# A gated linear attention with a channel mix on one core: the first two 128-token groups as one of 256, no separate load of the fourth head pair, and dummy products in the planned TensorE gaps up to the first mix

## The chip, the core and the metric

The kernel runs on one core of a Trainium2 chip. The metric is the device time of one execution in microseconds (us), the median of several runs. TensorE is called PE here (PEld is its weight load), VectorE DVE, ScalarE ACT, GpSimd POOL and SyncE SP. SP does no arithmetic here: it issues the transfers.

## What is computed

Two stages follow each other. The first is a recurrence over 768 tokens, for 4 sequences and 8 heads of 48 features, with a 48x48 state for each head:

```python
for t in range(S):
    state = alpha[:, :, t, :, None] * state + np.einsum('bhd,bhe->bhde', k[:, :, t], v[:, :, t])
    y[:, :, t] = np.einsum('bhd,bhde->bhe', q[:, :, t], state)
```

The second takes y with the heads side by side as x (4, 768, 384) and mixes each token with the one before it:

```python
xk = mu_k * x + (1.0 - mu_k) * x_prev
xr = mu_r * x + (1.0 - mu_r) * x_prev
k = np.maximum(xk @ w_k, 0.0)          # 384 -> 1024
v = k * k @ w_v                        # 1024 -> 384
out = 1.0 / (1.0 + np.exp(-(xr @ w_r))) * v
```

## The kernel before, in words

**Groups and chunks.** A sequence is cut into chunks of C = 128 tokens, and the chunks into attention groups (`CUTS`, L29). Before, the first sequence is cut 1, 1, 2, 2 and the others 2, 2, 2, so there are 13 groups and 24 chunks. `PLACE` (L32) says in which of two buffers a group's alpha, q, k and v lie and at which half of it: the two one-chunk groups share buffer 0. `MOES` (L34) says which groups one channel mix takes: the first mix takes groups 0 and 1 (256 columns), the second group 2 (256), the other five two groups each (512).

**Preparing a group** (`attention_inputs`, L313). SP loads alpha, q, k and v. DVE scans alpha forward for each head pair (`forth`, L364), multiplies q by the products (`times`, L391), takes a reciprocal (`turn`), scans backward (`back`, L406) and multiplies k. The rows hold three head pairs in full, and the fourth pair's 96 features lie as 16 further rows of each of the three. Group 0 alone is in `DIRECT` (L33): it has its fourth pair loaded once more into its own place (`extra`, L331, six transfers for alpha, q and k), and its scans run over four pairs. Every other group scans three pairs, and SP gathers the fourth pair of the finished q and k by transfers within the core's memory (`gather`, L428, two each, and `small`, L441, two for the decay at the group's end).

**Products of a chunk** (`attention_products`, L626). TensorE transposes k (`trans`), ACT copies it out (`keep`). For the first `JOINED` = 4 chunks the products come in two jobs: `enter` (state growth and scores, 64 + 64 instructions in the profile, which shows each float32 product as two) and, after DVE has masked the scores (`masked`) and advanced the state (`advance`), `visit` (output). Later chunks join the visit of one with the entry of the next. ACT copies the output (`leave`), DVE adds a part (`crossed`), and SP spreads the fourth pair (`spread`, L576).

**The channel mix.** `mix_jobs` (L861) forms xk and xr: for each of three feature blocks ACT scales, DVE blends, ACT rounds to a high part and DVE takes the low part. `up_jobs` (L894) makes eight products blocks, each of 9 PE products (high x high, low x high, high x low, three blocks each), and after each one ACT's `relu`, `square` and `whole` and DVE's `low`. `gate_jobs` makes three blocks of 9, `down_jobs` three of 24, closed by DVE and stored by SP. The up blocks, gates and downs of all mixes form one chain on PE in program order (`pe_job`, L890); only attention jobs can go between. In the first mix `up_jobs` is called for each of the two segments (L1007), so there are 16 up blocks of 128 columns, planned with a factor 1.6 (`slow`, L895); its gates and downs are 256 wide.

**Weights.** w_k, w_r and w_v come in 10 pieces through two raw buffers (`weights`, L729, `RAWS` = 2): SP loads (L739), ACT takes the top bits (L744), DVE joins (L752), ACT makes the high part (L760), DVE the low one (L764), and then the buffer is free for the piece after next.

**What sets the order.** Every step is a job of a `Plan` (L67) with a planned duration, and `plan.order` lists the jobs by planned start after 60 rounds of list scheduling. Each engine and SP then runs its own jobs in that order, whatever the true durations are. At the head of PE's stream 22 dummy products of zeros are issued (`WARM`, L52). While the planned start is below `QUIET` = 45 us, dummies also fill PE's planned gaps from the first job on:

```python
if plan.start[j] < QUIET and at > 0.0:
    for i in range(int((plan.start[j] - at - 0.2) / 0.2)):
        PE.matmul(pms[2][:R, :R], zero, zero, start=True, stop=True)
at = plan.start[j] + plan.dur[j]
```

A dummy is two PE instructions in the profile (L235 and L1057).

Of the kernel before, what the change touches and what calls it, by code (L numbers as in the profile page):

```python
# [25 lines left out]
B, H, S, D = 4, 8, 768, 48  # L26
DM, FF = 384, 1024
C = 128
CUTS = [[1, 1, 2, 2], [2, 2, 2], [2, 2, 2], [2, 2, 2]]  # L29
GROUPS = [(b, sum(cut[:i]), n) for b, cut in enumerate(CUTS) for i, n in enumerate(cut)]  # L30
NA = len(GROUPS)
PLACE = [(0, 0), (0, 1)] + [(i, 0) for i in range(1, NA - 1)]  # L32
DIRECT = (0,)  # L33
MOES = [[0, 1], [2], [3, 4], [5, 6], [7, 8], [9, 10], [11, 12]]  # L34
NG = len(MOES)
LMAX = 2 * C
WMAX = 2 * LMAX
NP = H // 2
# [4 lines left out]
NT = 3  # L43
# [5 lines left out]
DW = D // DQ  # L49
NX = HB - D  # L50
NW = 768
WARM = 22  # L52
ROUNDS = 60
RAWS = 2
JOINED = 4
QUIET = 45.0


def head(i, o):
# [120 lines left out]
def mm(n):  # L180
    return 0.013 + n / 2400.0 if n > 128 else 0.068
# [6 lines left out]
def act(n, extra=0.0):  # L188
    return 0.13 + n / 1200.0 + extra
# [7 lines left out]
def gated_attention_channel_mix(  # L197
# [17 lines left out]
    PE, ACT, DVE, POOL, SP = nc.tensor, nc.scalar, nc.vector, nc.gpsimd, nc.sync  # L215
# [21 lines left out]
    als, pps, ks, qs = (ring(x, 2, [128, NP * LMAX]) for x in ("al", "pp", "k", "q"))  # L237
    vs = ring("v", 2, [C, 2 * VW])
    for t in (als[0], ks[0], qs[0]):
        POOL.memset(t[:, NT * C : NP * C], 1.0)  # L240
    tiny = cp.tile([128, 1], F32, name="tiny")
    POOL.memset(tiny, FLOOR)
    mone = cp.tile([128, 1], F32, name="mone")
# [32 lines left out]
    tops = [early[:, :NW], *ring("tops", 1, [128, NW], U32)]  # L276
# [19 lines left out]
    plan = Plan()  # L296
    add = plan.add
# [12 lines left out]
    loads, prepped, gathered, half_k, half_q, rescale = {}, {}, {}, {}, {}, {}  # L310
# [150 lines left out]
    def final(a):  # L461
        return a + 1 == NA or GROUPS[a + 1][0] != GROUPS[a][0]

    def trans(i):
        a, c = CH[i]
        k = view(a, ks)
        for p in range(NT):
            PE.transpose(pt[:, p, :], k[:, p, c * C : (c + 1) * C], ident)  # L468
# [141 lines left out]
    def advance(i):  # L610
        a, c = CH[i]
        old, new, nxt = before[i, 0], before[i, 1], marks[i]
        DVE.tensor_tensor(by_pair(new), by_pair(old), grown[:R, 0], op=ALU.add)
        if nxt is None:
            return
        DVE.tensor_tensor(by_pair(nxt), by_pair(new), grown[:R, 1], op=ALU.add)
        if c == GROUPS[a][2] - 1:
            DVE.tensor_tensor(
                by_pair(nxt), by_pair(nxt), pes[a % 2][:R].unsqueeze(2).to_broadcast([R, NP, D]),
                op=ALU.mult,  # L620
            )
# [4 lines left out]
    def attention_products():  # L626
        last_mask = last_leave = last_cross = last_adv = last_visit = None
        done = {}
        tcopy = {}

        def slow(i):
            return 1.3 if i < JOINED else 1.0

        def joined_at(i):
            return i >= JOINED

        for i in range(-1, NCH):
            more = i + 1 < NCH
            need = [last_mask, last_adv, last_leave, last_cross, last_visit]
            opened = ()  # L640
            if more:
                a, c = CH[i + 1]
                tr = add(
                    "PE", 0.32 * slow(i), lambda i=i: trans(i + 1), need=[prepped[a]],
                    takes=[("pt", i + 1)], uses=[("k", a)], name=f"trans{i + 1}",
                )

                def keep(i=i):
                    ACT.copy(hts[(i + 1) % 2].rearrange("t (r i) -> t i r", i=NT), pt)  # L649

                tcopy[i + 1] = add(
                    "ACT", act(NT * 128, -0.02), keep, need=[tr], takes=[("ht", i + 1)],
                    uses=[("pt", i + 1)], name=f"ht{i + 1}",
                )
                ready = [tcopy[i + 1], *half_k[a], *half_q[a], *loads[a]["v"]]
                touched = [("ht", i + 1), ("k", a), ("q", a), ("v", a)]
                opened = (0,) if marks[i + 1] is None else (0, 1)
            if i >= 0:
                mine = [("am", i), ("q", CH[i][0]), ("v", CH[i][0]), *before[i]]
            joined = i >= JOINED and more  # L660

            def visit(i=i, out=i >= 0, more=more, opened=opened if joined else ()):
                if more and joined_at(i):
                    update(i + 1, opened)
                if out:
                    intra(i, opened)
                    inter(i, 0)
                    inter(i, 1)
                if more and joined_at(i):
                    scores(i + 1)  # L670

            def enter(i=i, opened=opened):
                update(i + 1, opened)
                scores(i + 1)

            vis = None
            if i >= 0:
                need += ready if joined else []
                vis = add(
                    "PE", (2.28 if joined else 1.5) * slow(i), visit, need=need,  # L680
                    uses=mine + (touched if joined else []), name=f"visit{i}",
                )
                last_visit = vis
                a, c = CH[i]
                last_leave = add(
                    "ACT", 0.5, lambda i=i: leave(i), need=[vis], takes=[("xt", slot_of[a])], name=f"leave{i}"
                )
                last_cross = add(
                    "DVE", 0.42, lambda i=i: crossed(i), need=[vis, last_leave], uses=[("xt", slot_of[a])],
                    name=f"cross{i}",  # L690
                )
                done.setdefault(a, []).append(last_cross)
            if more and not joined:
                a, c = CH[i + 1]
                vis = last_visit = add(
                    "PE", 1.0 * slow(i), enter, need=[*ready, last_mask, last_adv, last_leave, last_cross, last_visit],
                    uses=touched, name=f"enter{i + 1}",
                )
            if more:
                last_mask = add(  # L700
                    "DVE", 0.62, lambda i=i: masked(i + 1), need=[vis], takes=[("am", i + 1)],
                    name=f"mask{i + 1}",
                )
                a, c = CH[i + 1]
                ending = c == GROUPS[a][2] - 1
                last_adv = add(
                    "DVE", 0.62 + (0.25 if ending and not final(a) else 0.0), lambda i=i: advance(i + 1),
                    need=[vis, last_adv, *(rescale.get(a, ()) if ending else ())],
                    takes=[("st", x) for x in held[i + 1]],
                    uses=[before[i + 1][0], *([("pe", a)] if ending else [])], name=f"state{i + 1}",  # L710
                )
            if i >= 0:
                a, c = CH[i]
                if c == GROUPS[a][2] - 1:
                    mv = add(
                        "SP", 0.2, lambda a=a: spread(a), need=done[a], uses=[("xt", slot_of[a])], name=f"spread{a}"
                    )
                    src = [] if GROUPS[a][1] == 0 else [done[a - 1][-1], xready[a - 1][0]]
                    pre = add(
                        "POOL", 0.25, lambda a=a: prefix(a), need=src, takes=[("xt", slot_of[a])],  # L720
                        uses=[("xt", slot_of[a - 1])] if src else [], name=f"prefix{a}",
                    )
                    xready[a] = [mv, *done[a], pre]


    converted = {}
    turn_w = [0]

    def weights(key, f, src, at, hi, lo):  # L729
        n = hi.shape[1] * hi.shape[2]  # L730
# [15 lines left out]
                raw.bitcast(BF16)[:, 4::4], AF.Copy,  # L746
            )

        hb = add("ACT", act(n), head_bits, need=[ld], takes=[("tops", i)], uses=[("raw", i)], name=f"top {key}{f}")

        def join():
            DVE.scalar_tensor_tensor(  # L752
# [139 lines left out]
        return j  # L892

    def up_jobs(g, n0, n, w, xr_):  # L894
        slow = 1.6 if g == 0 else 1.0  # L895
        for f in range(NF):
            i, pk = acc(n)
            ri = rn[0]
# [5 lines left out]
            def ops(f=f, pk=pk, r=r, k2=k2, dst=dst, xh=xh, xl=xl):  # L904
# [4 lines left out]

            prod, relu = up_ops(f, pk, xh, xl, r, k2, None, None)[:2]  # L910
            jp = pe_job(
                9 * mm(n) * slow, prod, [*xr_, *converted["k", f // 2]], takes=[("pm", i)], uses=[("xk", g)],
                name=f"up{g}.{f}+{n0}",
            )
            jr = add("ACT", act(n, -0.02), relu, need=[jp], takes=[("r", ri)], uses=[("pm", i)], name=f"relu{g}.{f}")
# [131 lines left out]
    for j in late:  # L1047
        plan.need[j] += [k for i in range(turn_w[0]) for x in ("tops", "raw") for k in plan.users[x, i]]

    todo = plan.order(sizes, ROUNDS)  # L1050
    POOL.tensor_scalar(nu, mu, -1.0, 1.0, op0=ALU.mult, op1=ALU.add)
    at = 0.0
    for j in todo:
        if plan.eng[j] == "PE":
            if plan.start[j] < QUIET and at > 0.0:
                for i in range(int((plan.start[j] - at - 0.2) / 0.2)):
                    PE.matmul(pms[2][:R, :R], zero, zero, start=True, stop=True)  # L1057
            at = plan.start[j] + plan.dur[j]
        plan.fn[j]()
    order.close()  # L1060

# [177 lines left out]
```

## Time and profile before

| what | us |
|---|---|
| median of 3 runs | 366.55 (364.83 to 367.21) |
| the profiled execution | 367.48 |
| its span, first to last instruction | 365.8 |
| PE busy in the span | 347.4 |
| DVE busy | 225.3 |
| ACT busy | 203.1 |
| start of the first up product | 33.57 |
| start of the first down product | 77.65 |

The profile shows one execution. Its times run from the span's start, and "busy" is the time in which an engine had an instruction in work. The granted clock is the share of TensorE's full speed that the chip gave: 1.00 is 2.4 GHz and 0.50 is 1.2 GHz.

### The profile page before, as it was taken

Reading aid. Unit: us, or ns where it says so; the run is one execution under the profiler, and the core shown is the slowest. Engines: PE = TensorE matmul, PEld = TensorE weight load, DVE = VectorE, ACT = ScalarE, POOL = GpSimd, SP = SyncE. Lnnn points to the kernel's source line nnn. Section 1 sums busy time; section 2 is a strip of 40 time slices with the busy share of each in tenths; the row PEclk is TensorE's granted clock in tenths of the full one; section 3 lists DMA queues with packets and bytes.
Section 4 is the critical chain, followed back from the end, with each engine's and each line's share of the span. In section 5 each row is a group of like instructions: output and inputs, shape, how many; then the busy total and the mean of one; then the engine's idle time right before and its main releaser. Section 6 shows DMA issues by size and latency. Waiting matters only on the chain. (4 is left out here: it accounts for less than half of the span.)

```text
span 365.8 us, 10482 instructions
## 1 busy us (share of the span) xinstructions
PE 347.4 (95%) x4469; PEld 301.1 (82%) x4469; DVE 225.3 (62%) x453; ACT 203.1 (56%) x405; POOL 24.6 (7%) x63
## 2 busy tenths in 40 slices
PE   7497999999999999999999999999999999999991
PEld 7387999999999888888888888888888888888780
DVE  5897566587898954659934679517479312743000
ACT  2756565455874993318981349951269731787100
POOL 6110021010000300100000010000000000000000
PEclk9798555599999999999999999999999999999997
DMA  5997705243644202543203443005421001100011
GB/s 182 319 316 227 232 2 185 55 143 82 175 112 125 77 6 62 161 161 90 78 3 104 135 142 110 18 2 126 144 68 39 2 3 42 40 29 0 4 59 35
DMA packets 18295, 35.62 MB, mean 97 GB/s; under 512 B 3776, under 2 KB 9408, under 8 KB 18240
## 3 DMA queue, kind: packets, MB, share of 16 engines
q1 hardware_dynamic: 18096, 34.86, 31.6%
q8 instruction: 37, 0.61, 0.7%
q14 instruction: 18, 0.15, 0.2%
q10 hardware_dynamic: 144, 0.00, 0.0%
HBM read 26.69 MB, written 4.72 MB: 86 GB/s over the span
## 5 line engine op out<-in xcount | busy, mean ns | idle before, releaser
L810 PE MATMUL pm<-xkh,wkh 128*128 128x512 f32 (+2 forms) x192 | 52.5, 388 | 1.6 <-ACT xkh L796 1.6
L810 PE MATMUL pm<-xkl,wkh 128*128 128x512 f32 (+2 forms) x192 | 51.5, 383 | 0.0
L810 PE MATMUL pm<-xkh,wkl 128*128 128x512 f32 (+2 forms) x192 | 51.5, 383 | 0.0
L810 PEld LDWEIGHTS pm<-xkh,wkh 128*128 128x128 f32 x192 | 37.6, 223 | 7.2 <-ACT xkh L796 2.0
L847 PE MATMUL pm<-kb,wvh 128*128 128x512 f32 x120 | 42.2, 404 | 0.0
L810 PEld LDWEIGHTS pm<-xkl,wkh 128*128 128x128 f32 x192 | 38.0, 224 | 4.9
L810 PEld LDWEIGHTS pm<-xkh,wkl 128*128 128x128 f32 x192 | 38.1, 224 | 4.9
L816 ACT ACTIVATE r<-pm 128x512 f32<-128x512 f32 (+2 forms) x64 | 31.1, 486 | 18.4 <-PE pm L810 18.1
L847 PE MATMUL pm<-kha,wvh 128*128 128x512 f32 (+1 forms) x108 | 38.1, 353 | 0.0
L847 PE MATMUL pm<-kla,wvh 128*128 128x512 f32 (+1 forms) x108 | 37.0, 342 | 0.0
L847 PE MATMUL pm<-kha,wvl 128*128 128x512 f32 (+1 forms) x108 | 36.8, 341 | 0.0
L790 ACT ACTIVATE x<-xt,mu 128x512 f32<-128x512 f32 (+2 forms) x48 | 26.3, 609 | 18.4 <-DMA xt<-xt 17.6
L582 DVE TENSOR_TENSOR am<-sp,mask 128x512 f32<-128x512 f32 x24 | 16.5, 688 | 31.6 <-PE sp L497 31.5
L822 ACT ACTIVATE k<-r 128x512 f32<-128x512 f32 (+2 forms) x64 | 32.6, 516 | 1.5 <-DVE kla L825 1.0
L649 ACT COPY ht<-pt 128x384 f32<-128x384 f32 x24 | 16.3, 678 | 30.3 <-PE pt L468 30.2
L793 DVE SCALAR_TENSOR_TENSOR x<-xt,nu,x 128x512 f32<-128x512 f32 (+2 forms) x48 | 27.3, 612 | 5.7 <-ACT x L790 4.9
L825 DVE TENSOR_TENSOR kb<-k,kb 128x512 fp32r<-128x512 f32 x20 | 13.8, 692 | 24.4 <-ACT k L822 14.9
L560 ACT COPY xt<-yu 112x512 f32<-112x512 f32 x24 | 14.0, 584 | 24.6 <-PE yu L535 20.5
L847 PEld LDWEIGHTS pm<-kb,wvh 128*128 128x128 f32 x120 | 22.6, 188 | 5.1
L970 DVE TENSOR_TENSOR sig<-pm,sig 128x512 f32<-128x512 f32 (+1 forms) x21 | 12.8, 611 | 22.3 <-PE pm L847 17.4
L409 DVE TENSOR_TENSOR_SCAN pp<-al,pp 128x255 f32<-128x255 f32 (+1 forms) x40 | 26.3, 690 | 0.3
L365 DVE TENSOR_TENSOR_SCAN pp<-al,tiny 128x256 f32<-128x256 f32 (+1 forms) x40 | 23.6, 630 | 3.3 <-DMA al<-al_p 1.7
(90 smaller groups left out, 630.4 us busy)
## 6 DMA issues: line engine op xcount, KB each, us to landing
v<-v_p SPq DMA_DIRECT2D x11, 400.0 KB, 5.1
al<-al_p SPq DMA_DIRECT2D x11, 384.0 KB, 3.2
q<-q_p SPq DMA_DIRECT2D x11, 384.0 KB, 3.8
k<-k_p SPq DMA_DIRECT2D x11, 384.0 KB, 3.7
out<-sig SPq DMA_DIRECT2D x15, 256.0 KB, 2.1
early<-wk_p SPq DMA_DIRECT2D x4, 768.0 KB, 4.5
early<-wv_p SPq DMA_DIRECT2D x4, 768.0 KB, 4.8
q<-q SPq DMA_DIRECT2D x22, 48.0 KB, 2.3
```

What stands on the lines that cost most here:

```text
L365: DVE.tensor_tensor_scan(view(a, pps)[:, p], view(a, als)[:, p], tiny.to_broadcast([128, n]), initial=START, op0=ALU.mult, op1=ALU.max,)
L409: DVE.tensor_tensor_scan(pp[:, p, 0 : n - 1][:, ::-1], x, x, initial=pp[:, p, n - 1 : n], op0=ALU.mult, op1=ALU.bypass,)
L560: ACT.copy(x[:R].rearrange("r i (s t) -> r i s t", s=2), yu[:R, :, : NP * HC].rearrange("r s (i t) -> r i s t", i=NP),)
L582: DVE.tensor_tensor(ams[i % 2], sp[:, :, : NP * HC].rearrange("c j (p t) -> c j p t", p=NP), mask.unsqueeze(1).unsqueeze(1).to_broadcast([ ...
L649: ACT.copy(hts[(i + 1) % 2].rearrange("t (r i) -> t i r", i=NT), pt)
L790: ACT.activation(x, now, AF.Copy, scale=mu[:, i, t : t + 1])
L793: DVE.scalar_tensor_tensor(x, prev, nu[:, i, t : t + 1], x, op0=ALU.mult, op1=ALU.add)
L810: PE.matmul(pk, w[:, t, cols], x[:, t], start=part == 0 and t == 0, stop=part == 2 and t == NT - 1,)
L816: ACT.activation(r, pk, AF.Relu)
L822: ACT.activation(k2, r, AF.Square)
L825: DVE.tensor_tensor(lo, k2, hi.bitcast(F32), op=ALU.subtract)
L847: PE.matmul(pv, w[f // 2][:, f % 2, cols], x, start=f == 0 and i == 0, stop=f == NF - 1 and i == 2,)
```

## The change

All four sequences are cut 2, 2, 2, so there are 12 groups, each of 256 tokens and each with a buffer half of the ring to itself. No group loads its fourth pair separately; group 0 gathers it as the others do. The first mix takes group 0, the second group 1, the rest two each. The first mix therefore calls `up_jobs` once, with 8 blocks of 256 columns. 20 dummies stand at the head. After them dummies fill every planned gap of PE, from planned time 8.6 on and with 0.19 us planned for one, up to the first job that writes the third accumulator (`filled`; the third up block of the first mix). Some planned durations change.

```diff
-CUTS = [[1, 1, 2, 2], [2, 2, 2], [2, 2, 2], [2, 2, 2]]
+CUTS = [[2, 2, 2]] * 4
-PLACE = [(0, 0), (0, 1)] + [(i, 0) for i in range(1, NA - 1)]
-DIRECT = (0,)
-MOES = [[0, 1], [2], [3, 4], [5, 6], [7, 8], [9, 10], [11, 12]]
+PLACE = [(i, 0) for i in range(NA)]
+DIRECT = ()
+MOES = [[0], [1], [2, 3], [4, 5], [6, 7], [8, 9], [10, 11]]
-WARM = 22
+WARM = 20
+WARMED = 8.6
-QUIET = 45.0
-        POOL.memset(t[:, NT * C : NP * C], 1.0)
+        POOL.memset(t[:, NT * LMAX :], 1.0)
-                    "PE", 0.32 * slow(i), lambda i=i: trans(i + 1), need=[prepped[a]],
+                    "PE", 0.26 * slow(i), lambda i=i: trans(i + 1), need=[prepped[a]],
-                    "ACT", act(NT * 128, -0.02), keep, need=[tr], takes=[("ht", i + 1)],
+                    "ACT", 0.61, keep, need=[tr], takes=[("ht", i + 1)],
-                    "DVE", 0.62 + (0.25 if ending and not final(a) else 0.0), lambda i=i: advance(i + 1),
+                    "DVE", 0.75 + (0.3 if ending and not final(a) else 0.0), lambda i=i: advance(i + 1),
-        hb = add("ACT", act(n), head_bits, need=[ld], takes=[("tops", i)], uses=[("raw", i)], name=f"top {key}{f}")
+        hb = add("ACT", act(n, 0.2), head_bits, need=[ld], takes=[("tops", i)], uses=[("raw", i)], name=f"top {key}{f}")
-        slow = 1.6 if g == 0 else 1.0
-                9 * mm(n) * slow, prod, [*xr_, *converted["k", f // 2]], takes=[("pm", i)], uses=[("xk", g)],
+                9 * mm(n), prod, [*xr_, *converted["k", f // 2]], takes=[("pm", i)], uses=[("xk", g)],
+    filled = set(plan.first["pm", 2])
-    at = 0.0
+    at = WARMED
+    cold = True
     for j in todo:
         if plan.eng[j] == "PE":
-            if plan.start[j] < QUIET and at > 0.0:
-                for i in range(int((plan.start[j] - at - 0.2) / 0.2)):
+            if cold:
+                for i in range(int((plan.start[j] - at) / 0.19)):
                     PE.matmul(pms[2][:R, :R], zero, zero, start=True, stop=True)
             at = plan.start[j] + plan.dur[j]
+            cold = cold and j not in filled
```

## Rows read from the trace of the kernel before

**Rows 1.** The page: busy time of each engine (share of the span, instructions), and the granted clock in 40 slices of 9.1 us, in tenths.
```profile
PE 347.4 (95%) x4469; PEld 301.1 (82%) x4469; DVE 225.3 (62%) x453; ACT 203.1 (56%) x405; POOL 24.6 (7%) x63
...
PEclk9798555599999999999999999999999999999997
```
**Rows 2.** Windows: the stretch, its length, then busy time and instructions of each engine in it, the granted clock, the busy share of the DMA engines and GB/s.
```profile
33.57:72.06 38.49, 38.49 (x344) 37.78 (x345) 24.57 (x64) 23.24 (x75) 3.67 (x3) 0.50 0.42 131
72.06:74.50 2.44, 2.44 (x12) 2.44 (x13) 1.80 (x2) 1.47 (x5) 0.00 (x0) 0.50 0.61 161
...
33.57:77.65 44.08, 44.08 (x435) 43.17 (x436) 28.72 (x70) 27.20 (x85) 3.67 (x3) 0.54 0.40 124
77.65:130.00 52.35, 52.13 (x870) 49.17 (x869) 47.73 (x101) 36.31 (x82) 6.63 (x9) 1.00 0.44 120
130.00:160.00 30.00, 30.00 (x560) 24.85 (x563) 15.17 (x31) 13.67 (x24) 1.27 (x4) 1.00 0.31 87
```
**Rows 3.** Timeline of PE in the first 34 us: start, length, what, and in brackets the idle time before it and what ended it.
```profile
14.58 0.87 PE L468 MATMUL pt<-ident,k 128*128 128x128 f32 x3 [6.50 <-DVE k L393]
...
16.22 0.97 PE L485 MATMUL yu<-v,ht 64*64 64x48 f32 x30
...
18.07 2.88 PE L1057 MATMUL pm<-zero 112*112 112x112 f32 x18
...
22.58 2.52 PE L1057 MATMUL pm<-zero 112*112 112x112 f32 x24
25.03 0.78 PE L485 MATMUL yu<-v,ht 64*64 64x48 f32 x30
...
27.79 0.34 PE L497 MATMUL sp<-q,k 48*64 48x64 f32 x6 [1.11 <-DMA k<-k]
...
30.89 1.04 PE L1057 MATMUL pm<-zero 112*112 112x112 f32 x8
33.57 0.91 PE L810 MATMUL pm<-xkh,wkh 128*128 128x128 f32 x3 [1.64 <-ACT xkh L796]
```
**Rows 4.** Timeline of PE, three products to a row: two neighbouring rows 128 columns wide, two 256 wide soon after, and two 256 wide later. The difference of two starts is what three products cost.
```profile
34.27 0.84 PE L810 MATMUL pm<-xkh,wkl 128*128 128x128 f32 x3
34.91 0.84 PE L810 MATMUL pm<-xkl,wkh 128*128 128x128 f32 x3
...
72.81 0.84 PE L835 MATMUL pm<-xrh,wrl 128*128 128x256 f32 x3
73.45 0.84 PE L835 MATMUL pm<-xrl,wrh 128*128 128x256 f32 x3
...
95.96 0.52 PE L810 MATMUL pm<-xkl,wkh 128*128 128x256 f32 x3
96.32 0.52 PE L810 MATMUL pm<-xkh,wkh 128*128 128x256 f32 x3
```
**Rows 5.** Timeline of PE: the entry of one chunk and what follows it, at 0.50 and at 1.00 of the clock.
```profile
47.76 0.97 PE L485 MATMUL yu<-v,ht 64*64 64x48 f32 x30
...
49.62 0.90 PE L810 MATMUL pm<-xkh,wkh 128*128 128x128 f32 x3
...
82.94 0.79 PE L485 MATMUL yu<-v,ht 64*64 64x48 f32 x30
...
84.22 0.38 PE L847 MATMUL pm<-kha,wvh 128*128 128x256 f32 x1
```
**Rows 6.** Groups by form: busy time, mean ns of one. The first two are of 33.57 to 79.01, the next of 79 to 113 on DVE and of 85 to 113 on ACT; the last two are timeline rows of ACT.
```profile
L822 ACT ACTIVATE k<-r 128x128 f32<-128x128 f32 x16 | 4.6, 301 | 0.0
...
L825 DVE TENSOR_TENSOR kla<-k,kha 128x128 fp32r<-128x128 f32 x16 | 4.3, 284 | 0.3 <-ACT k L822 0.3
...
L825 DVE TENSOR_TENSOR kla<-k,kha 128x256 fp32r<-128x256 f32 x8 | 3.2, 414 | 0.0
...
L822 ACT ACTIVATE k<-r 128x256 f32<-128x256 f32 x8 | 3.3, 409 | 1.1 <-DVE kla L825 1.0
...
30.86 0.96 ACT L790 ACTIVATE x<-xt,mu 128x128 f32<-128x128 f32 x3
...
84.56 1.31 ACT L790 ACTIVATE x<-xt,mu 128x256 f32<-128x256 f32 x3 [3.64 <-DMA xt<-xt]
```
**Rows 7.** The start. Timeline of SP (one of the three pairs of fourth-pair loads, then a gather of k), windows as in rows 2, and from the view of one line the times from issue to landing (least, median, most) up to 60 us, first of the gathers of q and k (L431), then of the spread (L579).
```profile
1.72 1.33 SPq L334 DMA_DIRECT2D al<-al_p  x2
...
21.57 1.21 SPq L431 DMA_DIRECT2D k<-k  x2
...
1.50:6.00 4.50, 4.50 (x26) 4.50 (x25) 2.05 (x6) 1.50 (x4) 4.16 (x19) 1.00 0.56 132
6.00:30.00 24.00, 16.24 (x294) 14.97 (x296) 20.15 (x39) 12.28 (x18) 3.92 (x8) 0.86 0.94 315
...
DMA to landing us min/median/max: 2.1/4.4/5.6
...
DMA to landing us min/median/max: 2.7/4.6/6.5
```
**Rows 8.** Timeline of DVE: forward and backward scans of one 256-token group, three pairs each.
```profile
77.86 1.85 DVE L365 TENSOR_TENSOR_SCAN pp<-al,tiny 128x256 f32<-128x256 f32 x3
...
100.69 2.02 DVE L409 TENSOR_TENSOR_SCAN pp<-al,pp 128x255 f32<-128x255 f32 x3
```
**Rows 9.** Waits of SP's queue: who was waited for, us in total, times, longest.
```profile
SPq L739 <- DVE wvl L764: 15.0, 2, 13.6
```

## The prediction

> **What bounds the kernel now.** I read the page first. PE is busy in 95% of the span, DVE in 62% and ACT in 56% [rows 1], so the whole asks for PE; but the line of the granted clock shows a hole. From slice 4 to slice 8, some 34 to 74 us, PE ran at the lower of its two clocks, 1.2 for 2.4 GHz [rows 1]. Then I cut that stretch out by windows. From 33.57 to 72.06 PE is busy in every one of 38.49 us at a clock of 0.50, and to 77.65 it has no idle time at all, while DVE is busy 28.72 and ACT 27.20 of 44.08 us [rows 2]. So this stage is bound by PE, and by a slow one. From 77.65 to 130 PE is full at 1.00, but DVE is busy 47.73 of 52.35 us, 91% [rows 2]: a second bound stands close behind the first. From 130 on DVE is half idle and PE full [rows 2].
>
> Then PE's timeline of the start. PE waits 6.50 us for the prepared k before its first transposes at 14.58, 1.11 for a gathered k, and 1.64 for the mixed input, which ends at the first up product at 33.57 [rows 3]. After 33.57 every us taken from PE's stream moves the end, as long as DVE, ACT and the transfers keep up.
>
> Last, the price of one product. The 128-wide ones start 0.64 us apart in threes (34.27 to 34.91), 0.213 each; the 256-wide ones at the same half clock also 0.64 (72.81 to 73.45), 0.213 each; at full clock the 256-wide cost 0.36 for three (95.96 to 96.32), and some 0.117 each [rows 4]. Half the width saved nothing. That is the row on which most of the forecast stands.
>
> **The change, part by part.** The sum is made against the profiled execution, 367.48, which lies 0.9 above the median of the runs, 366.55; I take the 0.9 off at the end.
>
> *Up products of the first mix.* Before: 16 blocks of 9, 144 products by 0.213 = 30.7 us. After: 8 blocks of 9, 72 products. At the half clock they cost 15.4, which saves 15.4 whatever the clock does. At full clock they cost 72 x 0.117 = 8.4, which saves another 7.0.
>
> *Clock for the rest of the stretch.* Of the 38.49 us, 38.49 - 30.7 = 7.8 are attention products and transposes. A chunk's entry takes 1.86 at 0.50 (47.76 to 49.62) and 1.28 at 1.00 (82.94 to 84.22) [rows 5], so 7.8 becomes 7.8 x 0.69 = 5.4: saves 2.4. The 2.44 us of gates at the half clock [rows 2] hold about 11 products, which save 0.096 each: 1.1.
>
> Whether the clock is full there is the open point. In the rows it fell to 0.50 at the first mix, after PE had stood idle for 1.64 us, and stayed there while PE was 100% busy with 128-wide products; it rose at 74.50, 2.4 us after the first 256-wide products at 72.06 [rows 2 to 4]. After the change all products of the mix are 256 wide and dummies fill the planned gaps ahead of it, so I take 1.00. Were it to fall again in an unplanned wait, the same row says some 2.4 us of 256-wide work until it is back, and half of that lost, 1.2 us. The Trainium skill (TensorE: Matmul & The Clock Gate, Part 1) has the halved clock as the default and sustained activity as what lifts it. The trace disagrees in 38 us of unbroken activity at 0.50 and agrees from 72.06 on; by the rule as it stands the clock would come back by itself and the sum stays as here, by the stretch alone it would be the third case below.
>
> So PE gives 15.4 + 7.0 + 2.4 + 1.1 = 25.9.
>
> *What loses its cover.* ACT and DVE had 44.08 us between the first up and the first down product; PE now needs 44.08 - 25.9 = 18.2. Of ACT's 27.20, relu and both squarings fall from 16 x 3 at about 0.30 to 8 x 3 at 0.41, 14.4 to 9.8 [rows 6]. The nine mix pieces in the stretch become three wide ones, as the first mix has one segment: the scaling 3 x 0.96 to 1.31 [rows 6], the rounding nine of 0.30 to three of 0.41, together 3.1 less. ACT needs 27.2 - 4.6 - 3.1 = 19.5. At 91% (DVE's density above, the highest of the two engines over such a stretch in these rows) that is 21.4, so 3.2 us late. DVE: 28.72, less 16 x 0.284 - 8 x 0.414 = 1.2 for the rests [rows 6] and some 3.5 for the mix: 24.0, or 26.4 at 91%, 8.2 late if all of it were wanted before the downs. It is not: it holds the preparation of later groups, and by 160 DVE has (28.72 + 47.73 + 15.17 - 4.7) = 86.9 of work against 100.5 of PE [rows 2]. Bounds 0 and 8.2; I take 3, near ACT's figure, since ACT's work there is wanted at once. The weights lie in the same hole: two raw buffers, a piece loaded again only when DVE's low part is done, and SP waited 13.6 us for that once [rows 9]; the last pieces of w_v must now be done some 24 us earlier.
>
> *The start.* Gone: six fourth-pair issues, two in 1.33 us, and in the 4.5 us in which most of them ran the transfers moved 132 GB/s, against 315 from 6 to 30 us [rows 7]. Gone too are the scans of a fourth pair. Added: group 0's alpha, q and k are twice as long, and q, k and the decay are gathered, each two issues in 1.2 us on SP's queue, behind which the next loads stand. By the rows: alpha there at 3.9 (an estimate: twice the bytes of now), scans 1.85 and 2.02 [rows 8], q, the reciprocal and k between and behind them some 2.3 (an estimate too), so k ready near 10.1, before the 14.58 of now if its load is there; its gather 1.2 and 4.4 (2.1 to 5.6) [rows 7], so the first entry at 15.7 (13.4 to 16.9, and 1 more if weight joins stand before it on DVE) against 16.22 [rows 3]. From there both chunks of the group must pass before the mix, whereas now chunk 0 is spread and mixed while chunk 1 is worked on. A chunk takes 30.89 - 25.03 - 1.11 = 4.8 [rows 3]; two 9.5, copy and add of their outputs about 1 each, the spread's issues 1.2 and landing 4.6 (2.7 to 6.5) [rows 7], the mix (33.57 - 30.86) x 1.36 = 3.7 [rows 3, 6]: 21.0. First up product at 36.7, 3.1 later than now; bounds 32.5 and 40.8. As the planner may put the next group's products into that wait, I take 2, with bounds -3 and 7.
>
> The Trainium skill (DMA: Bandwidth & Descriptors, Anatomy of one DMA) puts a transfer's fixed cost at about 2.0 us. The least gather agrees with 2.1, the median of 4.4 does not; by the page the gather and the spread would be 5 us shorter together and the sum 5 less.
>
> *Dummies.* Each is 2 instructions: 9 took 2.88 us at the low clock, 0.32 each, and 12 took 2.45 (22.58 to 25.03) at full, 0.20 each [rows 3], against 0.19 planned. They stand in PE's own queue, so the chunk's products behind them wait for them. With some 19 us of gaps ahead of the mix, 100 dummies overrun by 1 us when warm, inside the start's bounds, and by 13 if they all ran cold.
>
> Sum: 367.5 - 25.9 + 3 + 2 = 346.6, less 0.9: 345.7.
>
> **The rivals.** *Nothing is given back.* ACT and DVE use their old idle time fully, the start comes out even: 367.5 - 25.9 - 0.9 = 340.7. For it: DVE has 38% idle over the span; against it: 91% right after.
>
> *The clock stays low through the first mix.* This is also the case in which the dummies don't do what they are for, because the gaps of the chip are not the planned ones. Only 15.4 is saved, PE needs 28.7 there and covers ACT and DVE: 367.5 - 15.4 + 2 - 0.9 = 353.2. For it: one idle time of 1.64 us stood before the fall, and the wait for the spread is longer after. Against: the rise at 74.50 under just such products.
>
> *ACT, DVE and weights become the bound, and the start is late*, both at their upper ends: 367.5 - 25.9 + 8.2 + 7 - 0.9 = 355.9.
>
> *Slower: SP's queue.* The gathers of group 0 and its spread stand in one queue with the weight loads, which wait for a raw buffer, up to 13.6 us [rows 9]. If a gather of k comes to stand behind such a wait, the first mix comes 13.6 later; with two such waits in the chain 27.2, and 345.7 + 27.2 = 372.9. It decides from 21 us on. Against: on the chip before, the gather waits cost PE 1.1 [rows 3].
>
> **How the numbers follow.** The forecast 0.56, its own range 341 to 351; nothing given back 0.18; low clock 0.13; both bounds 0.09; SP's queue 0.03; and 0.01 for cold dummies, which with the low clock end at 353.2 + 13 = 366, no change. The range 338 to 356 takes the low-clock case and most of the next, and at the lower end the case without loss with a start up to 3 us earlier. About 1% (3.7 us) is what a measurement can tell from no change here: faster by more 0.95, within 0.02, slower 0.03.
>
> **What would show it.** 72 up products 256 wide in the first mix, 0.35 to 0.36 us for three; a clock line without its run of fives; the first up product between 32 and 40 us and the first down product near 55 to 58, not 77.65; on PE from there to 130's place a few us of waits for ACT or DVE, where now there are none. The forecast is wrong if the clock reads 0.50 through the first mix, if PE waits more than 8 us between the first up product and the end of the first downs, or if the mix starts after 41.

## The result, and the profile after

The changed kernel takes 349.14 us in the median (347.92 to 349.47, 4 runs) beside 366.88 for the kernel before: a ratio of 0.9517, with a 95% interval of 0.9468 to 0.9565. Forecast were 345.7 and, from 366.55, a gain of 20.9; measured is a gain of 17.7. The profiled execution took 347.92, the fastest of the four, with a span of 346.1. In later series, 1 to 4 of 7 to 11 executions of the kernel before took 358 to 360 at a mean granted clock of 0.95 and not 0.93 (probably with the full clock in part of the first mix, but no trace shows such an execution), against which the changed kernel gains some 9 to 10 us; its medians below are over all executions.

The page: the run of fives in the clock line of [rows 1] is gone.
```profile
PE 330.5 (95%) x4493; PEld 283.9 (82%) x4493; DVE 220.6 (64%) x421; ACT 197.0 (57%) x367; POOL 19.8 (6%) x60
...
PEclk9899999999999999999999999999999999999998
```
Windows from the span's start to the first up product (41.00), to the first down product (56.75), and two about as long as the last two of [rows 2] behind it; the columns are those of [rows 2].
```profile
0.00:41.00 41.00, 35.04 (x611) 33.42 (x611) 31.61 (x55) 22.47 (x36) 8.47 (x36) 0.96 0.80 268
41.00:56.75 15.75, 15.21 (x230) 14.37 (x231) 15.68 (x32) 15.11 (x36) 0.00 (x0) 1.00 0.73 234
56.75:109.10 52.35, 49.42 (x974) 46.88 (x973) 43.80 (x94) 33.65 (x79) 4.64 (x9) 1.00 0.38 108
109.10:139.00 29.90, 29.90 (x356) 24.66 (x355) 18.02 (x35) 17.20 (x32) 1.67 (x4) 1.00 0.28 77
```
The first down product comes 20.9 us earlier than the 77.65 of before, in a stretch where PE (15.21 of 15.75), DVE (15.68) and ACT (15.11) are all full. From it to the span's end it is 289.4 us, against 288.2 before: 1.2 are given back. So 19.7 of span is the gain of these two executions.

PE's timeline up to the first mix, to be read beside [rows 3] and [rows 4]; the last rows are neighbouring threes of 256-wide products, the first down product, two waits and the first down product of the third mix.
```profile
12.93 0.87 PE L468 MATMUL pt<-ident,k 128*128 128x128 f32 x3 [2.85 <-DVE k L393]
13.60 3.15 PE L1058 MATMUL pm<-zero 112*112 112x112 f32 x18
...
17.59 0.79 PE L485 MATMUL yu<-v,ht 64*64 64x48 f32 x30
...
31.80 0.78 PE L485 MATMUL yu<-v,ht 64*64 64x48 f32 x30
...
36.13 0.69 PE L513 MATMUL yu<-am,v 64*64 64x64 f32 x32
...
41.00 0.62 PE L810 MATMUL pm<-xkh,wkh 128*128 128x256 f32 x3 [1.96 <-ACT xkh L796]
...
46.06 0.50 PE L810 MATMUL pm<-xkh,wkh 128*128 128x256 f32 x3
46.40 0.50 PE L810 MATMUL pm<-xkh,wkl 128*128 128x256 f32 x3
...
56.75 0.31 PE L847 MATMUL pm<-kha,wvh 128*128 128x256 f32 x1
...
71.46 0.50 PE L810 MATMUL pm<-xkh,wkh 128*128 128x256 f32 x2 [1.28 <-ACT xkh L796]
...
91.25 0.77 PE L485 MATMUL yu<-v,ht 64*64 64x48 f32 x29 [1.65 <-ACT ht L649]
...
128.66 0.39 PE L847 MATMUL pm<-kha,wvh 128*128 128x512 f32 x1
```
Three 256-wide products now cost 0.34 (46.06 to 46.40), where [rows 4] had 0.64 in the first mix and 0.36 later. The first chunk enters at 17.59 (16.22 before [rows 3]) and the mix starts at 41.00 (33.57 before), but the third chunk's entry (31.80) and output (36.13) are done ahead of it, which before came after.

### The profile page after: what moved, and what is told of

Read it like the earlier page. It is cut to its first block, busy times and chain, and to the rows that moved or that the text cites. A ratio compares the mean times of both kernels' runs of the same rounds, so it can differ in the third digit from the quotient of the medians.

```text
span 346.1 us, 10420 instructions
## 1 busy us (share of the span) xinstructions
PE 330.5 (95%) x4493; PEld 283.9 (82%) x4493; DVE 220.6 (64%) x421; ACT 197.0 (57%) x367; POOL 19.8 (6%) x60
## 5 line engine op out<-in xcount | busy, mean ns | idle before, releaser
L810 PE MATMUL pm<-xkh,wkh 128*128 128x512 f32 (+1 forms) x168 | 43.4, 365 | 3.2 <-ACT xkh L796 3.2
L790 ACT ACTIVATE x<-xt,mu 128x512 f32<-128x512 f32 (+1 forms) x42 | 25.2, 654 | 30.8 <-DMA xt<-xt 30.8
L810 PE MATMUL pm<-xkl,wkh 128*128 128x512 f32 (+1 forms) x168 | 42.2, 359 | 0.1
L810 PE MATMUL pm<-xkh,wkl 128*128 128x512 f32 (+1 forms) x168 | 42.1, 359 | 0.0
L847 PE MATMUL pm<-kha,wvl 128*128 128x512 f32 (+1 forms) x108 | 36.7, 340 | 0.0
L810 PEld LDWEIGHTS pm<-xkh,wkl 128*128 128x128 f32 x168 | 29.2, 188 | 5.0
L822 ACT ACTIVATE k<-r 128x512 f32<-128x512 f32 (+1 forms) x56 | 31.5, 564 | 2.6 <-DVE kla L825 1.8
L816 ACT ACTIVATE r<-pm 128x512 f32<-128x512 f32 (+1 forms) x56 | 29.4, 530 | 6.1 <-PE pm L810 5.7
L793 DVE SCALAR_TENSOR_TENSOR x<-xt,nu,x 128x512 f32<-128x512 f32 (+1 forms) x42 | 26.5, 668 | 4.8 <-ACT x L790 4.4
L825 DVE TENSOR_TENSOR kb<-k,kb 128x512 fp32r<-128x512 f32 x20 | 13.8, 691 | 23.3 <-ACT kb L819 12.6
L365 DVE TENSOR_TENSOR_SCAN pp<-al,tiny 128x256 f32<-128x256 f32 x36 | 22.8, 674 | 5.1 <-DMA al<-al_p 2.6
L409 DVE TENSOR_TENSOR_SCAN pp<-al,pp 128x255 f32<-128x255 f32 x36 | 25.1, 735 | 0.5 <-DVE pp L402 0.2
```

The costliest lines, as they stand in the source:

```text
L365: DVE.tensor_tensor_scan(view(a, pps)[:, p], view(a, als)[:, p], tiny.to_broadcast([128, n]), initial=START, op0=ALU.mult, op1=ALU.max,)
L409: DVE.tensor_tensor_scan(pp[:, p, 0 : n - 1][:, ::-1], x, x, initial=pp[:, p, n - 1 : n], op0=ALU.mult, op1=ALU.bypass,)
L790: ACT.activation(x, now, AF.Copy, scale=mu[:, i, t : t + 1])
L793: DVE.scalar_tensor_tensor(x, prev, nu[:, i, t : t + 1], x, op0=ALU.mult, op1=ALU.add)
L810: PE.matmul(pk, w[:, t, cols], x[:, t], start=part == 0 and t == 0, stop=part == 2 and t == NT - 1,)
L816: ACT.activation(r, pk, AF.Relu)
```

## The experiments

All times are medians. Three series had the kernel before beside them, at 366.0, 366.3 and 365.6 (one execution of 646.7 in the third moves its median by 0.3); a fourth, of one kernel, at 364.5.

**Without the dummies in the gaps.**
```diff
             if cold:
-                for i in range(int((plan.start[j] - at) / 0.19)):
-                    PE.matmul(pms[2][:R, :R], zero, zero, start=True, stop=True)
```


> The changed kernel without the dummies in the gaps; the 20 at the head stay. Theory (the width of the products gives most of the gain, the dummies little): the clock is low in part of the first 41 us, but the 256-wide products bring it back within some 3 us of the first mix, so 349 to 353 us. Rival (the dummies hold the clock and give most of it): the clock stays at 0.50 through the first mix as it did before, 356 us or more.


349.4 (348.49 to 350.29): no different from the changed kernel, and in the theory's band. PE's and ACT's timelines, then windows:
```profile
15.19 0.97 PE L485 MATMUL yu<-v,ht 64*64 64x48 f32 x30
...
36.96 0.51 ACT L790 ACTIVATE x<-xt,mu 128x256 f32<-128x256 f32 x1 [3.47 <-DMA xt<-xt]
...
40.13 1.01 PE L810 MATMUL pm<-xkh,wkh 128*128 128x256 f32 x3 [1.68 <-ACT xkh L796]
```
```profile
15.00:40.13 25.13, 14.08 (x392) 11.80 (x390) 21.43 (x41) 14.50 (x26) 2.39 (x5) 0.50 0.83 271
40.13:44.50 4.37, 4.37 (x28) 4.14 (x32) 4.37 (x10) 4.37 (x8) 0.00 (x0) 0.50 0.51 173
44.50:45.50 1.00, 1.00 (x64) 1.00 (x60) 1.00 (x2) 1.00 (x4) 0.00 (x0) 0.84 0.39 72
45.50:56.90 11.40, 11.40 (x159) 11.10 (x151) 10.55 (x22) 9.97 (x26) 0.00 (x0) 1.00 0.79 247
```
Without dummies PE runs at 1.2 GHz from 15 us on, and the mix still starts at 40.13: ACT waits 3.47 us for the spread (xt) first, and PE then for ACT. Under the 256-wide products the clock is back at 2.4 GHz some 5 us later, not the 3 expected, with no dummies. The rival, that the dummies give most, fell for the changed kernel.

**The dummies alone.** The kernel before with the new fill:
```diff
-WARM = 22
+WARM = 20
+WARMED = 8.6
-            if plan.start[j] < QUIET and at > 0.0:
-                for i in range(int((plan.start[j] - at - 0.2) / 0.2)):
+            if cold:
+                for i in range(int((plan.start[j] - at) / 0.19)):
```


> The kernel before with the dummies of the change alone (20 at the head, gaps filled from planned time 8.6 up to the third up block); groups, loads and 128-wide products as before. Theory: the clock falls again under the 128-wide products, so 364 to 368 us, no change. Rival: dummies hold the clock at 1.00 into the first mix and it stays there, 345 to 352 us.


359.3 (358.81 to 359.87), between the two: a miss for both. It is 6.7 below the median of the kernel before in its series, but not below the lowest execution of it there, 358.16. PE's timeline and windows:
```profile
33.23 0.50 PE L811 MATMUL pm<-xkh,wkl 128*128 128x128 f32 x3
33.57 0.50 PE L811 MATMUL pm<-xkl,wkh 128*128 128x128 f32 x3
...
45.06 0.55 PE L811 MATMUL pm<-xkh,wkh 128*128 128x128 f32 x3 [1.80 <-ACT r L817]
```
```profile
32.85:46.40 13.55, 11.74 (x154) 11.30 (x155) 11.94 (x34) 11.86 (x39) 0.32 (x1) 1.00 0.73 241
46.40:48.00 1.60, 1.60 (x16) 1.48 (x19) 1.60 (x4) 1.60 (x6) 1.00 (x1) 0.53 0.04 10
48.00:60.00 12.00, 12.00 (x167) 11.65 (x163) 7.74 (x24) 8.13 (x29) 2.49 (x2) 0.50 0.46 141
```
The clock is carried into the 128-wide products, and at 1.00 they too cost 0.34 for three (33.23 to 33.57), the price of 256-wide ones. It lasts 13.5 us and falls 1.3 us after the end of a wait of 1.80; it then reads 0.50 through the unbroken 128-wide work behind. That the wait makes it fall is not shown: the changed kernel held the full clock after waits of 1.96 and, in another execution, 2.50.

**The changed kernel with half the width.**
```diff
-                up_jobs(g, n0, n, w, mix_jobs(g, 0, n0, n, w, [a]))
+                mixed = mix_jobs(g, 0, n0, n, w, [a])
+                for h0 in range(n0, n0 + n, C):
+                    up_jobs(g, h0, C, w, mixed)
```


> The changed kernel with the first mix's up products cut back to 128 columns, 16 blocks of 9 on the same group of 256 tokens; all else as changed. Theory: a 128-wide product costs as much as a 256-wide one and the clock falls under them as before, so the first mix is some 20 to 25 us longer: 367 to 374 us, clock at 0.50 in it. Rival 1 (the clock is held, only the count doubles): 8 us longer, 355 to 359. Rival 2 (the products are not what it is about, the start and the other engines are): 348 to 352.


370.85 (367.45 to 373.62), as the theory had it: 21.7 over the changed kernel by the width alone, and more than the kernel before. PE's timeline and one window:
```profile
39.90 0.50 PE L810 MATMUL pm<-xkh,wkl 128*128 128x128 f32 x3
40.23 0.49 PE L810 MATMUL pm<-xkl,wkh 128*128 128x128 f32 x3
...
42.23 0.84 PE L810 MATMUL pm<-xkh,wkl 128*128 128x128 f32 x3
42.87 0.84 PE L810 MATMUL pm<-xkl,wkh 128*128 128x128 f32 x3
```
```profile
44.00:72.00 28.00, 28.00 (x265) 27.41 (x266) 11.68 (x28) 11.60 (x43) 0.19 (x1) 0.50 0.41 129
```
With the dummies in place the clock fell some 2 us after the first 128-wide product, ahead of which PE had waited only 0.84, and stayed low while PE was 100% busy.

**The width alone.** The kernel before, its up products run once over both segments:
```diff
-        slow = 1.6 if g == 0 else 1.0
...
-                9 * mm(n) * slow, prod, ...
+                9 * mm(n), prod, ...
...
-            gates = []
+            gates, mixed = [], []
...
-                up_jobs(g, n0, n, w, mix_jobs(g, 0, n0, n, w, [a]))
+                mixed += mix_jobs(g, 0, n0, n, w, [a])
                 gates += mix_jobs(g, 1, n0, n, w, [a])
                 n0 += n
+            up_jobs(g, 0, w, w, mixed)
```


> The kernel before (its 13 groups, its separate fourth-pair load and its own dummies) with one thing of the change: the first mix's up products run once over 256 columns when both segments are mixed, 8 blocks of 9, planned without the factor 1.6. Theory (the width is the change): the first up product some 4 to 7 us later than before, the clock back within 3 us of it, the whole gain there: 347 to 353 us. Rival (regrouping and dummies carry part of it): 355 to 361.


354.32 (352.76 to 355.11) beside 365.6: 11.3 less, just above the theory's band and just below the rival's. Its first up product came at 44.31, 10.7 later than before, where 4 to 7 were expected. Windows from there to the first down product at 62.92:
```profile
44.31:47.00 2.69, 2.69 (x14) 2.69 (x13) 1.95 (x3) 1.59 (x6) 0.19 (x1) 0.50 0.55 143
47.00:62.90 15.90, 14.83 (x284) 14.02 (x282) 13.28 (x30) 13.63 (x36) 0.10 (x1) 0.98 0.47 154
```
So the width is the larger part, some 11 us. The other 4 to 5 fit the downs, which start at 56.75 in the changed kernel and not at 62.9. What moves them was not tested by itself: as the run without gap dummies, and the one with the fourth pair below, change the time little, the grouping by 256 from the start and the planned durations are what is left.

**The fourth pair loaded again.**
```diff
-DIRECT = ()
+DIRECT = (0,)
```


> The changed kernel with group 0's fourth pair loaded separately again (six more transfers, scans over four pairs, no gather for group 0). Theory (the start lies on the path, and the gather of k is in it): the six issues and a fourth scan cost some 2 us, the gather saved gives back 3 to 5, so the first entry comes 1 to 3 us earlier and the time is 346 to 349. Rival (leaving out the separate load was a gain): 351 to 354.


349.93 (348.87 to 350.58): both missed. The start was no earlier: transposes at 15.59 instead of 12.93, first up product at 44.55, first down product at 61.65, 4.9 late. Yet by the medians the end is 0.8 late, within the scatter. In the two traced executions it is 2.7 late (spans of 348.8 and 346.1), so at least 2.2 of the 4.9 are given back later, which is what the next runs were for.

**The changed kernel again, and mu first.** mu's load is moved ahead of ACT's table load:
```diff
+    mu = cp.tile([128, 2, NT], F32, name="mu")
+    nc.scalar.dma_start(mu, mu_p)
     gone = cp.tile([128, 1], F32, name="gone")
     ACT.activation(gone, ones, AF.Sigmoid)
-    mu = cp.tile([128, 2, NT], F32, name="mu")
-    nc.scalar.dma_start(mu, mu_p)
```


> The changed kernel again, as the measure for the three runs beside it: 348 to 350 us.

> The changed kernel with the small load of mu issued ahead of ACT's table load instead of behind it; PE's, DVE's, POOL's and SP's orders are the same. In the changed kernel POOL's nu waits 1.89 us for mu, and with it the ends of the first scans and DVE's reciprocal (1.37 us idle). Theory A (the start is on the path to the end): the first up product comes 1 to 1.4 earlier, and so does the end: 347.5 to 348.3. Theory B (an earlier mix meets DVE and ACT, which are full from 41 to 60, and its gain is lost there): no change beyond 0.4 us.


350.26 (348.46 to 350.42) again, 0.3 above its band, and 349.27 (348.19 to 351.29) with mu first: between A and B, and not settled. The up products came at 40.77, but in that execution the clock fell for 3 us under them.

**A late mix.**
```diff
+            if j == plan.first["pm", 1][0]:
+                for i in range(14):
+                    PE.matmul(pms[2][:R, :R], zero, zero, start=True, stop=True)
         plan.fn[j]()
```


> The changed kernel with 14 more dummies (2.9 us at 0.204 each) in PE's queue between the first and the second up block of the first mix; every order else is the same. Theory A (PE bounds everything after the first up product): the whole 2.9 us stand in the end, 351.5 to 352.5. Theory B (DVE and ACT stand close behind: PE waits 1.28 and 1.65 us for them at 71 and 91): the two waits swallow the delay, 0 to 1.2 us later than the changed kernel.


350.44 (349.4 to 352.62), 0.2 over the changed kernel beside it. PE's timeline, first of this run (its slowest execution, 352.62), then of the changed kernel beside it (349.09), to the first down products of the first and of the third mix:
```profile
43.69 3.99 PE L1063 MATMUL pm<-zero 112*112 112x112 f32 x28
...
60.94 0.28 PE L847 MATMUL pm<-kha,wvh 128*128 128x256 f32 x1
...
133.50 0.39 PE L847 MATMUL pm<-kha,wvh 128*128 128x512 f32 x1
```
```profile
57.19 0.33 PE L847 MATMUL pm<-kha,wvh 128*128 128x256 f32 x1
...
130.15 0.39 PE L847 MATMUL pm<-kha,wvh 128*128 128x512 f32 x1
```
The medians are B. The traced executions are not: the first downs start 3.75 later, the third downs 3.35 later, and the end comes 3.5 later (352.62 against 349.09), so there little of the delay was swallowed. In that execution the clock was 0.50 from 43.0 to 45.9, which made the 14 dummies cost 3.99, and no trace shows one of the five faster executions. This run does not settle whether PE alone bounds what follows the first mix; the next two bear on it.

**No checks.**
```diff
+    POOL.memset(racc, -1.0)
...
-        add("ACT", act(NT * n, 0.2), check, need=took["al"], uses=[("al", a)], name=f"check{a}")
```


> The changed kernel without the 12 checks of alpha on ACT (1.1 us each; it leaves out the test that alpha is at most 1). Theory B (ACT is part of what holds the stretch from 41 to 100): 2 to 4 us less, 345 to 347, and the waits of 1.28 and 1.65 gone. Theory A (only PE's own work counts): under 1 us less.


348.24 (347.0 to 349.41), 2.0 less: at the small end of B's 2 to 4, and 1.2 above its band of times. As B said, the waits of 1.28 and 1.65 are gone (from 60 to 109 us PE idles 0.22), though PE waits 1.67 for ACT at 58.91. The changed kernel shows how 1.1 us of a check can matter. Its SP, PE and ACT timelines ahead of the wait at 91.25:
```profile
86.27 0.33 SPq L327 DMA_DIRECT2D al<-al_p  x1
...
87.75 0.49 PE L468 MATMUL pt<-ident,k 128*128 128x128 f32 x3
...
89.62 0.94 ACT L357 ACTIVATE junk<-al,mone 128x768 uint8<-128x768 f32 x1 [3.00 <-DMA al<-al_p]
...
90.55 0.65 ACT L649 COPY ht<-pt 128x384 f32<-128x384 f32 x1
```
The transposes are ready at 88.2, but ACT stands 3.00 us at a check whose alpha was issued at 86.27, and copies them only at 90.55.

**The checks later.** The check follows the group's finished k:
```diff
-        add("ACT", act(NT * n, 0.2), check, need=took["al"], uses=[("al", a)], name=f"check{a}")
...
         prepped[a] = km
+        add("ACT", act(NT * n, 0.2), check, need=[km], uses=[("al", a)], name=f"check{a}")
```


> The changed kernel with the check of each group's alpha on ACT made to follow the group's finished k instead of its load, so that ACT, which works in order, does not stand at a check whose load is late (2.3 and 3.0 us at 70 and 90, behind which a copy of transposed k was late and PE waited 1.65). Theory (the stretch from 57 to 110 is held by ACT and the chain of the chunks): 1 to 2.5 us less than the changed kernel beside the same runs of before, 347.5 to 349. Rival (it was the 1.1 us of ACT's work for each check, as without checks): no change.


346.87 (345.64 to 348.79): 2.3 to 3.4 below the two medians of the changed kernel, 0.6 better than the theory's band, and better than both kernels (in its series the kernel before was itself 0.7 to 1.3 lower than in theirs). Windows of it, the last from its first downs to the downs of its third mix, and then the same stretch of the changed kernel:
```profile
70.00:90.00 20.00, 19.74 (x476) 18.94 (x471) 17.43 (x42) 13.83 (x37) 0.91 (x3) 1.00 0.51 153
90.00:110.00 20.00, 20.00 (x285) 18.28 (x278) 17.33 (x33) 13.71 (x25) 0.42 (x3) 1.00 0.34 93
...
58.31:127.41 69.10, 68.84 (x1176) 62.90 (x1174) 54.77 (x115) 48.52 (x104) 5.68 (x10) 1.00 0.35 96
```
```profile
56.75:128.66 71.91, 68.98 (x1179) 62.97 (x1178) 55.91 (x118) 48.35 (x105) 5.19 (x10) 1.00 0.33 91
```
PE has the same 69 us of work in that stretch in both kernels; it idles 0.26 us here and 2.93 in the changed kernel. So there PE alone was not the bound. All 12 checks are still made, and ACT's waits for alpha in that stretch, 5.3 us in the changed kernel, are gone, so the time came from where ACT waited, not from its work. The plan also ordered other jobs otherwise, and the first downs come 1.6 later than in the changed kernel's first trace; what that alone does was not tested.

**The same on the kernel of the width alone** (the two diffs together).


> The kernel of the width alone with the checks moved as in the run before it. If both edits hold and add: 1 to 2.5 us under the width alone. Rival: the order of the plan changes more than the edits give, and it lies within 1 us of the width alone.


356.36 (355.32 to 358.94), 2.0 over the width alone: it did not add, and the rival's 1 us is missed too. Its PE waits 11.9 us for prepared k, 9.8 without the edit, which points to the plan's other order; no run tests it.

**Checks later and a late mix** (the two diffs together).


> The kernel with the checks moved, with the same 14 dummies (2.9 us) between the first and the second up block as in the late-mix run. In the kernel with the checks moved PE's trace has no wait above 0.3 us between the first up product and 130 us. Theory (that kernel is bound by PE from the first mix on, the changed kernel was not): now the 2.9 us stand in the end, 349 to 350.2 us, 2.2 to 3.3 over the 346.87 without them. Rival (the delay is swallowed wherever it falls, since DVE and ACT run behind PE there too): 346.9 to 347.9.


349.12 (347.55 to 351.97), 2.25 over the kernel with the checks moved. In the band of the theory, but the runs of the two overlap and are of different series. In their traces the mix starts 0.9 earlier than without the dummies (43.28, 44.16) and the third downs come 1.1 later (128.49, 127.41), so some 2.0 of the 2.9 stand: likely, not settled.

## Why the prediction was right, point by point

*The price of a product* held, and it is the cause. 144 products at 0.213 became 72 at 0.113 to 0.118. Half the width at the same cost is shown at both clock levels ([rows 4] and the 0.34 of the dummies-alone run), and cutting the width back alone loses the whole gain.

*The clock terms*, 7.0, 2.4 and 1.1, came in, but by another hand. I put them to 256-wide products and dummies together. The dummies alone take 6.7 off the median of the kernel before (366.0 to 359.3) and nothing once the products are wide: without them the mix ran at the low clock for some 4.5 us, against the 2.4 at which I had priced an unplanned fall, and ended no later. The clock rose after 2.4, 4.4 and 2.7 us of 256-wide products in three kernels (before, without gap dummies, width alone) and not in 28 us busy with 128-wide ones. The rule of the Trainium skill (TensorE: Matmul & The Clock Gate, Part 1) that sustained activity lifts the clock agrees with the first and not with the second.

*The start* was mis-sized: the first up product at 41.00, where I had 36.7 and at most 40.8. That is at the edge of my own sign of a wrong forecast, a mix that starts after 41, and the second trace of the changed kernel, at 41.46, is past it. The first entry was at 17.59 and not 15.7. These rows, of DVE, POOL and ACT, show what I had not counted:
```profile
7.95 0.21 POOL L1051 TENSOR_SCALAR nu<-mu 128x6 f32<-128x6 f32 x1 [1.89 <-DMA mu<-mu_p]
...
8.68 0.18 DVE L402 RECIPROCAL pp<-pp 128x3 f32<-128x3 f32 x1 [1.37 <-POOL pe L383]
...
10.20 0.93 DVE L752 SCALAR_TENSOR_TENSOR early<-early 128x768 uint32<-128x768 uint32 x1
...
19.15 0.68 DVE L582 TENSOR_TENSOR am<-sp,mask 128x512 f32<-128x512 f32 x1
...
22.13 2.02 DVE L409 TENSOR_TENSOR_SCAN pp<-al,pp 128x255 f32<-128x255 f32 x3
...
28.12 0.68 DVE L582 TENSOR_TENSOR am<-sp,mask 128x512 f32<-128x512 f32 x1
...
37.81 0.51 ACT L790 ACTIVATE x<-xt,mu 128x256 f32<-128x256 f32 x1 [3.37 <-DMA xt<-xt]
```
POOL, waiting for mu, held the decays and with them DVE back 1.37, a weight join stood 0.93 between two scans, and 9 dummies ran cold in 3.15 at 13.60. Two chunks then took 12.6 (17.59 to 30.15) instead of 9.5. The dummies are not the main cause: without them the first entry came at 15.19, but the first up product still at 40.13. What both runs share is DVE's queue: in the changed kernel the next group's scans (2.02 at 22.13) and k and three weight jobs stand between the masking of the first chunk's scores (19.15) and of the second's (28.12); that is read from the traces, and no run tests it. The spread and the mix took 10.9 (30.15 to 41.00) where 11.5 was worked out. Against that 2.7 of the third chunk's products went into the wait, so the net is 41.00 - 33.57 - 2.7 = 4.7, where I took 2 (within its bounds of -3 and 7). The 2.0 us that the prediction quotes from the Trainium skill (DMA: Bandwidth & Descriptors, Anatomy of one DMA) stands there for transfers that GpSimd issues; SP issues those here, and up to 60 us the gathers took 2.1, 3.2 and 6.5 (least, median, most).

*The lost cover*, 3, was put in the wrong place. Between up and down PE idled only 0.54 us, with DVE at 99.6% and ACT at 96%, above the 91% that I took as their limit. The two errors cancel there by luck: the downs came at 56.75, inside the 55 to 58 forecast. The loss came later, as waits of 1.28 and 1.65, and its mechanism was not one of mine: ACT, in order, standing at a check for a late load.

*The sum.* On the profiled execution 346.6 was forecast and 347.92 measured. The remaining 2 of the 3.4 lie in that execution being 1.2 below its own median, where I had assumed the 0.9 above of the kernel before.

## What to carry to other kernels

Read the price of a product from the start-to-start of two rows before counting columns: here 128 and 256 columns cost the same, so narrow products paid double, and for most of them the clock was low too. When one engine's stage is halved, look for the in-order waits on the other engines that the slow stage had hidden: moving a job that waits for a load behind another user of that load took 2.3 to 3.4 us here, though the same edit cost 2.0 on the kernel of the width alone. A delay put in on purpose can test whether an engine is still the bound, but then the trace and the time must be of the same execution: for the late mix the medians said 0.2 and the traced execution 3.5.

## What the runs showed that I had not expected

Through 28 us of unbroken 128-wide products the clock stayed at 1.2 GHz, yet a clock of 2.4 GHz lasted 13.5 us under them in one run and 2 us in another. What made it fall is open: PE had waited 1.80 and 0.84 ahead of these falls, and 1.96 and 2.50 in the changed kernel where it did not fall. In three other runs with 256-wide products (mu first, the late mix, no checks) it fell for some 3 us early in the mix and came back. And dummies that run at the low clock cost 0.35 each (3.15 us for 9), so filling by planned time delays the work behind them just when the clock is down: the first entry came at 17.59 with them and at 15.19 without.
